# Block-causal attention and a gated feed-forward layer: other halves of PSUM share a tile in the last two seven-product stages, and the written-out order is searched anew

## The chip, the cores and the metric

The kernel runs on one core of a Trainium2 chip. The metric is the device time of one execution in microseconds; before the change it is 959.42 us, the median of three runs (957.42 to 960.23). Engines are called as in the profile: PE is TensorE (matmuls; PEld its weight loads), DVE is VectorE, ACT is ScalarE, POOL is GpSimd, SP is SyncE, which only issues DMA transfers. SPq and ACTq are the issues of transfers on SP's and ACT's queues.

## The reference

Inputs are q, k, v of shape (8, 8, 576, 64), w_in (512 x 2048) and w_out (2048 x 512). The output has 4608 x 512 elements.

```python
scores = scale * np.matmul(q, k.transpose(0, 1, 3, 2))      # scale = 1/8
scores = np.where(block_i >= block_j, scores, -1e9)         # blocks of 64 positions
attn = np.exp(scores - np.max(scores, axis=-1, keepdims=True))
attn = attn / (np.sum(attn, axis=-1, keepdims=True) + 1e-09)
x = np.matmul(attn, v)         # then heads side by side: 4608 x 512
h = x @ w_in
sp = np.where(h > 20.0, h, np.log1p(np.exp(np.minimum(h, 20.0))))
g = h * np.tanh(sp)
out = g @ w_out
```

## The kernel before

The 4608 tokens are nine tiles of 512 (b = 0 to 8). For each pair of heads the scores are computed (line 1499), their maxima taken (1544), the exponentials (1580) split into an fp16 high and low part (1624, 1631), transposed by DMA (1659, 1674) and multiplied by v (1714); a divide (1780, 1781) ends the attention of a pair, and further transposes (1967) turn the result into x. The weights arrive as pairs of 32-bit words, and DVE decodes them (825, 842); w_out comes in 16 chunks (816). ACT squares it (854), a matmul with ones, `over_rows` (748), sums the squares over the rows, and the scale found from it goes into the fp16 parts wo_h and wo_l (890, 902).

Both feed-forward matmuls are made of three fp16 products (high by high, high by low, low by high). For tiles 4 to 8 the first of them is done with seven products of half size in place of eight, as in Strassen's scheme (`m1_set`, 2182); tiles 7 and 8 do the second one so too (`m2_seven`, 2363), the others plainly (2530). In the seven-product scheme some operands are sums (S1 to S4) of blocks and some are blocks (A11, A12, A22), and the results are added up in PSUM and SBUF.

`m2_seven` works with three accumulators of 128 x 512 fp32, each a PSUM bank: X for A11 and later A12, Y for S2, then S3, then A22, Z for S1, then S4. PSUM tiles named `ss` are two banks wide, and there are two of them: X and Y are the halves of one, Z is in the other. A11, S2 and S1 are computed in four sets of 24 matmuls each over the inner dimension. Then, in this order on PE, come A12, S3, S4 and A22 (two halves of 24 matmuls), 48 matmuls each. Between them stand small operations: X is copied (`w1`, on ACT at 2401 or DVE at 2407), the copy is added into Y (`a1`, 2416), Y is copied (`cu`), Z is copied (`w2`), Y's copy is added into Z (`a2`), and the copy of Z and Y are added (`a3`). S3 begins when `cu` is done, S4 when `a2` is. The results leave by `out`: a scaled evacuation on DVE (2470) or ACT (2464) and a store (2494). The last one, of tile 8, is split into a half for DVE and a half for ACT, with the second half's store on ACT's queue.

The order of the work on every engine is written out. `AT` holds a due time for each operation, `WAY` one letter for each operation that several engines can do ("a", "d", "p"). `Plan.go` goes through the operations by due time with the costs that each was added with (a model of SP's queue among them: BEGIN, DONE, FLIGHT), and `order` emits them by the starts found so, per engine. The Tile framework then adds the semaphores: an instruction that touches a tile waits for the earlier ones on that tile which it must follow. A buffer ring (`ss_ring`, `work_ring`, ...) says when a tile may be taken again.

Of the kernel before, what the change touches and what calls it, by code (L numbers as in the profile page):

```python
# [358 lines left out]
class Plan:  # L359
# [5 lines left out]


    LAT, LATPE, OWN = 0.15, 0.2, 0.11

    FREE = 0.4

    BEGIN, DONE, FLIGHT = 0.65, 1.6, 8

    SWITCH = 1.3

    WINDOW, COLUMNS, SLOW, LEAD = 10.24 / 3, 3400, 1.93, 0.5

    def __init__(self):
# [20 lines left out]
    def go(self, due):  # L398
# [15 lines left out]
        while events:  # L414
            now = events[0][0]
            while events and events[0][0] <= now:
# [3 lines left out]
                o = ops[i]  # L420
# [2434 lines left out]
```

## Time and profile before

| | before |
|---|---|
| median of 3 runs | 959.42 us (957.42 to 960.23) |
| profiled execution | 958.82 us |
| its span | 956.9 us |
| mean granted PE clock | 0.998 |
| busy: PE / DVE / ACT / POOL | 937.5 / 764.6 / 605.4 / 280.6 us |

The span runs from the first to the last recorded instruction or transfer of the profiled execution; its own time is 1.9 us longer. A busy share close to the whole says which engine sets the pace; which stretch a change acts on is to be seen from the stretches, the waits and the chain that ended last.

### The profile page before, as it was taken

To read this page: it belongs to the slowest core of one execution; us is meant where nothing else is said; L and a number is where in the kernel's file an instruction comes from. 1 tells how busy PE (TensorE), PEld (TensorE's weight loads), DVE (VectorE), ACT (ScalarE), POOL (GpSimd) and SP (SyncE) were. 2 spreads that over 40 slices of the span, in tenths; PEclk is the share of its full clock that TensorE was granted. 3 is DMA by queue.
4 is the path that set the end of the run, shared out by engine and by line. 5 is a ranking of instruction groups with operands and counts; after the bars stand their busy time and mean duration, and the time that the engine had idled before them with its cause. 6 is when DMAs were issued, how large, how long until landed. Compare 5 with 4: busy or idle time off the path is not lost.

```text
span 956.9 us, 22382 instructions
## 1 busy us (share of the span) xinstructions
PE 937.5 (98%) x9060; PEld 616.5 (64%) x9060; DVE 764.6 (80%) x1445; ACT 605.4 (63%) x1021; POOL 280.6 (29%) x267
## 2 busy tenths in 40 slices
PE   8999998999999999999999999999999999999997
PEld 6777574545554555555557865786568747888886
DVE  7889998878789887766988886899768788984861
ACT  2739997568737884597667964688569424631540
POOL 0001211323335132233333605422575502201320
PEclk9999999999999999999999999999999999999999
DMA  8762889776664568866677769766886440014001
GB/s 293 245 204 95 190 179 216 165 161 130 139 128 98 136 147 170 164 141 160 138 155 147 149 135 181 143 155 147 162 180 106 81 102 17 13 40 105 1 1 45
DMA packets 298472, 128.35 MB, mean 134 GB/s; under 512 B 244608, under 2 KB 280704, under 8 KB 298368
## 3 DMA queue, kind: packets, MB, share of 16 engines
q1 hardware_dynamic: 298080, 126.49, 59.7%
q8 instruction: 71, 1.16, 0.5%
q10 hardware_dynamic: 288, 0.43, 0.1%
q14 instruction: 33, 0.27, 0.1%
HBM read 58.06 MB, written 10.49 MB: 72 GB/s over the span
## 4 chain that ended last, share of the span: by engine, by line
PE 90%; DVE 6%; DMA 2%; ACT 2%; issue 1%; SPq 0%; ACTq 0%; DVEq 0%
PE acc L2530 29%; PE acc L2182 18%; PE acc L2091 15%; PE ss L2363 8%; PE acc L1714 6%; PE ss L1499 6%; PE acc L1429 3%; PE ss L1358 1%; DVE sx L842 1%; DVE P L1631 1%; PE ss L1286 1%; DMA PT<-P 1%; DVE pv L1544 1%; DVE Gt L2040 1%; PE acc L1286 1%; PE acc L927 1%
## 5 line engine op out<-in xcount | busy, mean ns | idle before, releaser
L2530 PE MATMUL acc<-Gt,wo_h 128*128 128x512 f16 x896 | 267.9, 381 | 0.1
L2530 PE MATMUL acc<-Gt,wo_l 128*128 128x512 f16 x448 | 170.4, 380 | 0.0
L1580 ACT ACTIVATE pe<-ss,pv 128x192 f32<-128x192 f32 (+2 forms) x240 | 126.3, 608 | 59.0 <-DVE pv L1554 37.9
L2091 PE MATMUL acc<-x,wi_h 128*128 128x512 f16 (+2 forms) x640 | 156.9, 337 | 1.1 <-DVE many L1781 0.9
L2530 PEld LDWEIGHTS <-wo_h 128*128 128x128 f16 x896 | 82.5, 98 | 92.7 <-issue 7.2
L1544 DVE TENSOR_REDUCE pv<-ss 128x2 f32<-128x384 f32 (+4 forms) x140 | 104.5, 790 | 25.1 <-PE ss L1511 24.3
L1631 POOL TENSOR_TENSOR P<-pe,P 128x256 f16<-128x256 f32 (+3 forms) x67 | 83.4, 1266 | 120.2 <-DVE P L1624 48.7
L2182 PE MATMUL acc<-x,wi_h 128*128 128x256 f16 x640 | 108.0, 273 | 0.0
L2040 DVE SCALAR_TENSOR_TENSOR Gt<-F,bv,Gt 128x1024 f16<-128x1024 f32 (+2 forms) x80 | 96.3, 1216 | 11.6 <-ACT Gt L2028 9.2
L2091 PE MATMUL acc<-x,wi_l 128*128 128x512 f16 (+2 forms) x320 | 104.6, 336 | 0.0
L2091 PEld LDWEIGHTS <-wi_h 128*128 128x128 f16 x640 | 56.9, 98 | 49.8 <-issue 3.0
L2182 PE MATMUL acc<-x,wi_l 128*128 128x256 f16 x320 | 87.2, 273 | 0.0
L2182 PE MATMUL acc<-x,sx 128*128 128x256 f16 x720 | 86.6, 273 | 0.3 <-DVE acc L2226 0.3
L1714 PEld LDWEIGHTS <-PT 128*128 128x128 f16 x2128 | 72.2, 97 | 11.0 <-issue 1.4
L2530 PEld LDWEIGHTS <-wo_l 128*128 128x128 f16 x448 | 44.0, 98 | 53.4 <-issue 0.8
L2182 PEld LDWEIGHTS <-sx 128*128 128x128 f16 x720 | 69.8, 98 | 10.2 <-issue 0.8
L1631 DVE TENSOR_TENSOR P<-pe,P 128x256 f16<-128x256 f32 (+3 forms) x101 | 73.4, 769 | 1.8 <-ACT P L1624 1.6
L1714 PE MATMUL acc<-many,PT 128*128 128x65 f16 (+1 forms) x2128 | 74.3, 193 | 0.0
L1499 PE MATMUL ss<-many 64*128 64x64 f16 (+7 forms) x1280 | 73.7, 260 | 0.1
L2182 PEld LDWEIGHTS <-wi_h 128*128 128x128 f16 x640 | 61.9, 98 | 11.6 <-issue 1.0
L760 POOL TENSOR_SCALAR Gt<-F,bv 128x1024 f16<-128x1024 f32 (+2 forms) x26 | 33.4, 1285 | 105.3 <-ACT F L2119 58.5
L2235 ACT ACTIVATE F<-acc,bv 128x512 f32<-128x512 f32 x60 | 40.5, 686 | 23.2 <-PE acc L2182 20.6
(245 smaller groups left out, 1681.7 us busy)
## 6 DMA issues: line engine op xcount, KB each, us to landing
wo_l<-in_w_in_dram SPq DMA_DIRECT2D x8, 1024.0 KB, 6.4
sx<-in_w_out_dram SPq DMA_DIRECT2D x16, 512.0 KB, 4.6
many<-in_v_dram SPq DMA_DIRECT2D x28, 288.0 KB, 3.1
many<-in_k_dram SPq DMA_DIRECT2D x28, 288.0 KB, 3.3
many<-in_q_dram SPq DMA_DIRECT2D x28, 256.0 KB, 3.3
out_dram<-ot SPq DMA_DIRECT2D x28, 256.0 KB, 2.9
many<-in_v_dram SPq DMA_DIRECT2D x28, 192.0 KB, 3.5
many<-in_v_dram SPq DMA_DIRECT2D x28, 96.0 KB, 3.1
```

The lines of the kernel that those rows point to most:

```text
L760: nc.gpsimd.tensor_scalar(out=out, in0=x, scalar1=s, scalar2=1.0, op0=ALU.mult, op1=ALU.mult)
L1499: nc.tensor.matmul(ss[:, 512 * a + col : 512 * a + col + n], lhsT=m[q_][hs, at : at + P], rhs=m[k_][hs, key : key + n], start=first, stop= ...
L1544: nc.vector.reduce_max(out=mx[:, c], in_=ss[:, :, c0:c1], axis=mybir.AxisListType.X)
L1580: nc.scalar.activation(pe[ex[r].slot][:, cols], ss_[S0[r].slot][:, cols], AF.Exp, scale=esc, bias=mx[:, c, a : a + 1],)
L1631: eng.tensor_sub(l, x, h)
L1714: nc.tensor.matmul(out, lhsT=p_, rhs=v_, start=first, stop=True, skip_group_check=True,)
L2040: nc.vector.scalar_tensor_tensor(out=dst[:, 1], in0=src, scalar=self.s_g, in1=dst[:, 0], op0=ALU.mult, op1=ALU.subtract,)
L2091: nc.tensor.matmul(pt, lhsT=w[:, d, f * P : (f + 1) * P], rhs=rhs(x, d), start=k == 0 and d == 0 and z == 0, stop=d == NP - 1 and z == 2, ...
L2182: nc.tensor.matmul(pt[:, k * TH : (k + 1) * TH], lhsT=weights(kind, z, d, k), rhs=x_[:, d, blk, x, :], start=first and k == 0 and d == 0 a ...
L2235: lambda: nc.scalar.activation(dst(), src(), AF.Mish, scale=scale),
L2363: nc.tensor.matmul(pt[:, k * TH : (k + 1) * TH], lhsT=weights(kind, z, s, c, k), rhs=block(blk, x, s, c), start=one, stop=s == NS - 1 and ...
L2530: nc.tensor.matmul(pt, lhsT=w[:, f, o * P : (o + 1) * P], rhs=g, start=s == 0 and c == 0 and z == 0, stop=s == NS - 1 and c == FG - 1 and ...
```

## The change

Four things are changed. The table `AT` and the string `WAY` are replaced as a whole by those of a new search. The plan's model lets a long transfer on SP (over 1.4 us of issue, which are the transposes) hold the queue until what was sent before it has landed, and some costs of the model are smaller (`TURN`, `TURN_LATE`, `TURN_X`, the 0.12 of `over_rows`, now 0.03); these numbers only steer the order. In `m2_seven` X and Z now share a tile and Y has its own; in the last of the four sets the order is S1, A11, S2; A12 also waits for Z's copy `w2`, `a2` for A12, and S4 for the evacuation of X; the rings are released accordingly, and both halves of the last result wait for the whole of A22. The instructions on PE are the same in number and kind (9060 matmuls).

```diff
-    0, 20114, 1050, 475, 0, 4150, 3025, 1425, 950, 6938, 1900, 4832, 5885, 23380, 7413, 15638,
+    0, 12977, 1050, 0, 475, 5885, 2375, 1900, 3025, 4832, 10683, 950, 9630, 23859, 23209, 15050,
...
-    "adaadaaddaddapaadpapaaaaapdddaadpaapaddaadppddddaaapadpdadddaadadpdaaaapdddpddddapdaddpaaa"
+    "adaadpaadpaaaadadadpaaaaaadddpaapadaaadaapppddddapapapadadpdaadpdpddadappdadadadddpaddpadd"
...
@@ -369,6 +369,8 @@
     FREE = 0.4
 
     BEGIN, DONE, FLIGHT = 0.65, 1.6, 8
+
+    QUEUED = 1.4
 
     SWITCH = 1.3
 
@@ -458,6 +460,8 @@
                     locked = until[e] = max(until[e] - ops[i].tail, locked) + ops[i].tail
                 end[i] = until[e]
                 if e == "sp":
+                    if us > self.QUEUED:
+                        until[e] = max(until[e], moved + self.DONE)
                     flight += 1
                     moved = max(moved, until[e] + self.BEGIN) + ops[i].work
                     end[i] = moved + self.DONE
@@ -753,7 +757,7 @@
                 stop=True,
             )
 
-        o = add("pe", (0.12, 10.0), emit, after, [acc_ring])
+        o = add("pe", (0.03, 10.0), emit, after, [acc_ring])
         return o, lambda: acc_[o.slot][:, 0:n]
 
     def by_pool(out, x, s):
@@ -2418,19 +2422,20 @@
                     psum=True,
                 )
 
-            bx, bz = [None, 0], [None, 0]
+            bx, by, bz = [None, 0], [None, 0], None
             ends = {"A11": last["m2"], "S1": last["m2"]}
             for s in range(NS):
-                for kind, blk, bank in (("A11", 0, bx), ("S2", 5, None), ("S1", 3, bz)):
+                order = (("A11", 0, bx), ("S2", 5, by), ("S1", 3, bz))
+                for kind, blk, bank in order if s < NS - 1 else order[::-2] + order[1:2]:
                     if bank is None:
-                        bank = [bx[0], 1]
-                        ends.setdefault(kind, ends["A11"])
+                        bank = bz = [bx[0], 1]
+                    ends.setdefault(kind, ends["A11"])
                     free = [(p2_ring, self.rooms[2])] if kind == "S2" and s == NS - 1 else []
-                    ends[kind] = product(
-                        0, kind, blk, (s,), s == 0, [ends[kind]], bank, free=free
-                    )
+                    after = [ends[kind]]
+                    if kind == "A11" and s == NS - 1:
+                        after.append(ends["S1"])
+                    ends[kind] = product(0, kind, blk, (s,), s == 0, after, bank, free=free)
             p1, p6, p5 = (ends[x] for x in ("A11", "S2", "S1"))
-            by = [bx[0], 1]
             X, Y, Z = bank_of(bx), bank_of(by), bank_of(bz)
             w2 = []
             t = many[:, 4 * TN : 6 * TN].rearrange("p (a n) -> p a n", a=2)
@@ -2440,18 +2445,11 @@
             w1 = copy(W1[0], X, [p1] + [x for m in self.more for ops in m for x in ops])
             a1 = plus(Y, Y, W1[0], [w1, p6])
             cu = copy(W1[1], Y, [a1])
-            p2 = product(1, "A12", 1, every, False, [w1], bx)
+            w2.append(copy(W2[1], Z, [p1, p5], [work_ring]))
+            p2 = product(1, "A12", 1, every, False, [w1, w2[0]], bx)
             p7 = product(1, "S3", 4, every, False, [cu], by, free=[(p2_ring, self.rooms[1])])
-            w2.append(copy(W2[1], Z, [p5], [work_ring]))
-            a2 = plus(Z, Z, W1[1], [cu, w2[0]])
+            a2 = plus(Z, Z, W1[1], [cu, w2[0], p2])
             a3 = plus(W2[1], Y, W2[1], [w2[0], p7])
-            p3 = product(2, "S4", 2, every, False, [a2], bz)
-            p4 = [product(3, "A22", 6, every, False, [a3, p3], by, (0,))]
-            rooms = [(ot_ring, self.rooms[0])]
-            p4.append(product(3, "A22", 6, every, False, [p4[0]], by, (1,), rooms))
-            self.m2_begin = p3
-            self.reads = NS * [[p3] + p4]
-            last["m2"] = p4[1]
             stored = []
             self.evacs = []
 
@@ -2502,12 +2500,19 @@
 
             both = range(2)
             out(1, 0, 0, both, X, W1[0], [p2, a1], True, [], [])
+            p3 = product(2, "S4", 2, every, False, [a2, self.evacs[0]], bz)
+            p4 = [product(3, "A22", 6, every, False, [a3, p3], by, (0,))]
+            rooms = [(ot_ring, self.rooms[0])]
+            p4.append(product(3, "A22", 6, every, False, [p4[0]], by, (1,), rooms))
+            self.m2_begin = p3
+            self.reads = NS * [[p3] + p4]
+            last["m2"] = p4[1]
             out(2, 1, 1, both, W2[1], W2[1], [a3], False, [], [])
-            out(3, 0, 1, both, Z, W1[1], [p3, a2], True, [(ss_ring, bz[0])], [])
+            out(3, 0, 1, both, Z, W1[1], [p3, a2], True, [(ss_ring, bx[0])], [])
             last["tail"] = [x + [stored[0], stored[2]] for x in last["tail"]]
             for k in range(2):
                 out(
-                    3, 1, 0, (k,), Y, W2[0], [p4[k]], True, [(ss_ring, bx[0])] * k,
+                    3, 1, 0, (k,), Y, W2[0], [p4[1]], True, [(ss_ring, by[0])] * k,
                     [(work_ring, w2[0])] * k,
                 )
 
@@ -2734,8 +2739,8 @@
         return top, lo
 
     SLACK = 0.7
-    TURN, TURN_LATE = (2.7, 0.5), (1.25, 0.2)
-    TURN_X = {8: (1.4, 0.5), 12: (2.0, 0.5), 16: (2.7, 0.5), 24: (3.8, 0.9)}
+    TURN, TURN_LATE = (2.0, 0.5), (1.2, 0.2)
+    TURN_X = {8: (1.3, 0.5), 12: (1.5, 0.5), 16: (2.0, 0.5), 24: (2.9, 0.9)}
     heads, tiles, fars = [[], []], [], []
 
     own = [load_own(p) for p in range(NP)]
```

How the instructions move is shown at three places. Lines of the changed kernel are 4 or 5 higher (2416 is 2420). The first place is DVE at the end of tile 8, from the last split of the gated activations on. `ss_128` and `ss_129` are the two PSUM tiles. Before:

```order
1301 L2040 SCALAR_TENSOR_TENSOR Gt<-F_64,bv_120,Gt 128x1024
1302 L2407 COPY F_65<-ss_129 128x2x256
1303 L2416 TENSOR_TENSOR ss_128<-ss_128,many 128x512
1304 L2416 TENSOR_TENSOR ss_129<-ss_129,many 128x512
1305 L2470 TENSOR_SCALAR many<-ss_128,bv_120 128x256 x2
1306 L2416 TENSOR_TENSOR F_65<-ss_128,F_65 128x2x256
1307 L2470 TENSOR_SCALAR F_65<-F_65,bv_120 128x256 x2
1308 L2470 TENSOR_SCALAR F_65<-ss_128,bv_120 128x256
```

And now:

```order
1295 L2044 SCALAR_TENSOR_TENSOR Gt<-F_65,bv_120,Gt 128x1024
1296 L2420 TENSOR_TENSOR ss_129<-ss_129,many 128x512
1297 L2411 COPY many<-ss_129 128x2x256
1298 L2420 TENSOR_TENSOR ss_128<-ss_128,many 128x512
1299 L2420 TENSOR_TENSOR F_64<-ss_129,F_64 128x2x256
1300 L2468 TENSOR_SCALAR F_64<-ss_129,bv_120 128x256
```

The sum `a1` (Y and the copy of X) was on `ss_128`, the tile in which A12 accumulates, and is now on `ss_129`; `a2` (1304, now 1298) has gone to the tile of X. X's evacuation (1305) has gone to ACT, and the copy `cu` (1297) has come from there.

The second place is SP while the last chunks of w_out are loaded (DMA into `sx`); DMA_TRANSPOSE into `PT` are the transposes of the exponentials. Before, from the 14th chunk to the 16th:

```order
78 L816 DMA sx_76<-in_w_out_dram 128x4x256
79 L1659 DMA_TRANSPOSE PT_107<-P_102 128x16x128
80 L980 DMA many<-in_v_dram 128x576
81 L1100 DMA many<-in_q_dram 128x2x64
82 L816 DMA sx_75<-in_w_out_dram 128x4x256
83 L1659 DMA_TRANSPOSE PT_108<-P_103 128x16x128
84 L816 DMA sx_76<-in_w_out_dram 128x4x256
```

And now:

```order
77 L1663 DMA_TRANSPOSE PT_107<-P_102 128x16x128
78 L820 DMA sx_76<-in_w_out_dram 128x4x256
79 L1124 DMA many<-in_v_dram 64x128
80 L984 DMA many<-in_v_dram 128x576
81 L1124 DMA many<-in_v_dram 64x3x128
82 L820 DMA sx_75<-in_w_out_dram 128x4x256
83 L1663 DMA_TRANSPOSE PT_108<-P_104 128x16x128
84 L820 DMA sx_76<-in_w_out_dram 128x4x256
```

The three chunks are the 14th, 15th and 16th in both. The transpose `PT_107` has moved from behind the 14th chunk to ahead of it, and three loads of v stand between 14th and 15th.

The third place is the end of SP's queue, the last stores of tile 8 (the last half store is on ACT's queue and not here). Before:

```order
448 L2494 DMA out_dram<-F_65 128x256
449 L2494 DMA out_dram<-F_65 128x2x256
450 L2494 DMA out_dram<-many 128x2x256
451 L2494 DMA out_dram<-F_65 128x256
452 L2494 DMA out_dram<-F_65 128x2x256
453 L2494 DMA out_dram<-F_65 128x256
454 L2494 DMA out_dram<-many 128x2x256 x2
```

And now:

```order
449 L2492 DMA out_dram<-F_66 128x256
450 L2492 DMA out_dram<-F_66 128x2x256
451 L2492 DMA out_dram<-F_66 128x256
452 L2492 DMA out_dram<-many 128x2x256
453 L2492 DMA out_dram<-F_64 128x2x256
454 L2492 DMA out_dram<-many 128x2x256
455 L2492 DMA out_dram<-F_64 128x256
```

The store of 128x256 (128 KB, a half of the last result) stood ahead of two stores of 128x2x256 (256 KB each, one row with x2) and is now the last one on SP.

## Rows read from the trace of the kernel before

**Rows 1.** The page's first line and part 1.

```profile
span 956.9 us, 22382 instructions
...
PE 937.5 (98%) x9060; PEld 616.5 (64%) x9060; DVE 764.6 (80%) x1445; ACT 605.4 (63%) x1021; POOL 280.6 (29%) x267
```

**Rows 2.** Waits of PE: engine, line, releaser, us, times, longest.

```profile
...
PE acc L748 <- ACT wo_h L854: 2.4, 1, 2.4
PE ss L2363 <- DVE ss L2416: 2.2, 1, 2.2
PE ss L2363 <- DVE many L2407: 1.6, 1, 1.6
PE ss L2363 <- ACT many L2401: 1.5, 1, 1.5
PE acc L2091 <- DVE many L1781: 0.9, 1, 0.9
```

**Rows 3.** Stretches: us, busy per engine (instructions), PE clock, DMA share, GB/s.

```profile
...
160.00:162.90 2.90, 0.50 (x3) 0.10 (x2) 2.76 (x8) 2.05 (x3) 0.00 (x0) 1.00 1.11 221
...
164.20:167.60 3.40, 3.40 (x9) 1.22 (x8) 3.19 (x7) 3.40 (x6) 0.00 (x0) 0.51 1.17 175
167.60:834.00 666.40, 665.94 (x6558) 405.71 (x6557) 545.45 (x1022) 444.51 (x770) 241.02 (x221) 1.00 0.65 134
```

**Rows 4.** Timeline, PE: start, us, engine, what, [idle before, releaser].

```profile
...
857.85 0.38 PE L2363 MATMUL ss<-many,wo_h 128*128 128x256 f16 x2 [1.59 <-DVE many L2407]
858.45 0.28 PE L2363 MATMUL ss<-many,wo_l 128*128 128x256 f16 x1 [0.23 <-DVE wo_l L2714]
...
865.82 0.38 PE L2363 MATMUL ss<-Gt,PT 128*128 128x256 f16 x2 [2.17 <-DVE ss L2416]
...
935.58 0.38 PE L2363 MATMUL ss<-many,wo_h 128*128 128x256 f16 x2 [1.48 <-ACT many L2401]
```

**Rows 5.** Chain that ended last, 920 to 957: start, us, what.

```profile
...
921.00 13.11 PE ss L2363 x120
...
934.21 0.71 DVE ss L2416
...
934.94 0.59 ACT many L2401
...
935.58 15.89 PE ss L2363 x144
```

**Rows 6.** Timeline, DVE, tile 7's seven-product stage.

```profile
...
863.69 0.88 DVE L2470 TENSOR_SCALAR many<-ss,bv 128x256 f32<-128x256 f32 x2 [2.42 <-PE ss L2363]
...
865.08 0.69 DVE L2416 TENSOR_TENSOR ss<-ss,many 128x512 f32<-128x512 f32 x1
```

**Rows 7.** The tail: timeline of issues, then issues with us to landing.

```profile
...
952.52 0.92 SPq L2494 DMA_DIRECT2D out_dram<-many  x2
952.58 0.36 ACTq L2494 DMA_DIRECT2D out_dram<-F  x1
...
out_dram<-many SPq DMA_DIRECT2D x2, 256.0 KB, 2.8
out_dram<-F SPq DMA_DIRECT2D x1, 128.0 KB, 1.8
out_dram<-F ACTq DMA_DIRECT2D x1, 128.0 KB, 2.5
```

**Rows 8.** Timeline, SP and then DVE, while w_out is loaded.

```profile
...
142.31 4.89 SPq L1659 DMA_TRANSPOSE PT<-P  x1
...
149.51 0.41 SPq L816 DMA_DIRECT2D sx<-in_w_out_dram  x1
...
153.81 0.52 SPq L816 DMA_DIRECT2D sx<-in_w_out_dram  x1
...
154.01 0.43 DVE L825 TENSOR_SCALAR sx<-sx 128x512 int32<-128x512 int32 x1 [2.45 <-DMA sx<-in_w_out_dram]
...
158.94 0.42 DVE L825 TENSOR_SCALAR sx<-sx 128x512 int32<-128x512 int32 x1
```

More of the change, by code (lines that the diff above doesn't have):

```diff
@@ L321 @@
 WAY = (
-    "adaadaaddaddapaadpapaaaaapdddaadpaapaddaadppddddaaapadpdadddaadadpdaaaapdddpddddapdaddpaaa"
-    "adaapppadapadpaadddpapdddpdpaddadpdaapaaapadadaaadppaaappadaaaapppdpdaddddaaadddapdaapddpd"
-    "ppdddaddpdpdadddddpdpdadaaapaddadpdadddadppapddpapdddaddpddpdpddpppddpdpdddapdddddddapddda"
-    "pdppddpaddddpdaaadpddapddpppddaddpdappdpdadpapadaddpadppadpadpdadappdpadaaddpaaddpdaaddada"
-    "adadaadaapdadadaapddaddpapddppdpdadapdapadppaappaappdddadppdpdpdaaadpdddpdadappadaapdaaaaa"
-    "padapapdadpdadpdppddapdddpppadppadpddappaadadadadappppapaaapadadapdaaapaadaadaaadpdadadapa"
-    "dpppapppapaadpddpdpapadpppppadpdppppdppaaaddddaddddppdpadddadddpadpddapddadddadpdpaddddddd"
-    "daddddddddaddddpdddadddadddpadaaadddapdpapaaddddapddaaaaaddpappddaaaadddaadaaaadaddaaddddd"
-    "ddadddpdpddddaaddppppadaaadpddapdpaadaddpdaapaapaaadddaadaapaaddda"
+    "adaadpaadpaaaadadadpaaaaaadddpaapadaaadaapppddddapapapadadpdaadpdpddadappdadadadddpaddpadd"
+    "ddaapapappdaaddaappddddddddddpdpddddadpapdadaddaapaaddaaddaddaaadddapddddaadapadapdaadddpd"
+    "pdpdddadppapapdpaaadaaapppdadadadddappdaddppppdpaddpdddddadddaddddppdppadppdddppddddappdpp"
+    "dpdaddpapppdadapaadapppdadadapadpdaapddppadpadddapapdddpaddadadaaapdddapdadpdaddppaadppada"
+    "daaaaaaadadpdaddaaadadapapdadpdpppppaddpddppadppaapddpddaaddddadadapddaddpdaaaaaadpaaadapd"
+    "pddapapddpapadddddaapddddpdaapppppppadapappddadadadppdddaaddpadapdddappdaadaaaaaapdpdapapa"
+    "dapadpappdaddppdpddaaadpppdpaadaddppdadadaddddadddpaddpddddpddpdaddddaddpddddadppdaddddadd"
+    "paddpddpddaddpdadddaddpaddddpdadaddddppaadaaddddaapaaadaadpdaapaaadaddddaadaaaaaaddddadapd"
+    "ppaddaddppdpaadpddaadppadaadpdapdpaaaadpddaapadpaaadddaapdaaadaaaa"
 )
```

566 rows, old and new, of the table AT are left out of this document.

## The prediction, made before the changed kernel was run

> **What bounds the kernel now.** I read the page first: a span of 956.9 us in which TensorE is busy for 937.5, 98% [rows 1]. TensorE is therefore the bound, and the whole room is what it does not spend at its full pace: 19.4 us idle, plus whatever it loses to a lower clock. Other engines matter where TensorE waits for them. The list of TensorE's waits [rows 2] puts the idle time down to few places: three waits of the seven-product stage (line 2363) for a sum or a copy, 2.2, 1.6 and 1.5 us; one of 2.4 at line 748, where the sum over w_out's rows waits for ScalarE's squares; one of 0.9 at line 2091 for a divide; the rest is below half a microsecond each, but for the wait for the first load of q, which opens the span. The table of stretches [rows 3] then says where in time that is: between 167.6 and 834.0, 70% of the span, TensorE is busy 665.94 of 666.40 us, so nothing is to be had there; around 160 to 168 there is first a gap and then 3.4 us at a granted clock of 0.51, the lower level of 1.2 GHz.
>
> **The waits of the seven-product stage.** Their size at the start of the next matmul is more than the idle column, since the ends of pipelined matmuls are modelled: a 128x256 matmul alone is booked as 0.27, and in a pair as 0.38, so the step is 0.11 (13.11 us for 120 in the chain [rows 5] gives 0.109). Each wait thus costs its idle time plus 0.27 - 0.11 = 0.16: 1.59 + 0.16 = 1.75 at 857.85, 0.23 + 0.16 = 0.39 at 858.45, 2.17 + 0.16 = 2.33 at 865.82, 1.48 + 0.16 = 1.64 at 935.58 [rows 4]. The sum is 6.1 us.
>
> What makes them is read in the chain around 934 [rows 5]. TensorE runs 120 matmuls up to 934.12; the last 48 are the product A12, which adds into X. Only then does VectorE's sum into Y start (934.21, 0.71 us), then ScalarE's copy (934.94, 0.59), and then S3 (935.58). The operands of that sum were complete when A12 began, 48 x 0.109 = 5.2 us earlier. It waited because X and Y are halves of one PSUM tile: the framework holds a reader or writer of a tile for the last writer of the tile, not of the half. Tile 7 has it the same way, and there again in front of S4: X's evacuation waits 2.42 us at 863.69 although A12 ended at 856.3 (857.85 less the 1.59 idle ahead of it [rows 4]), because S3 writes Y in the same tile; the sum into Z at 865.08 stands behind it on VectorE [rows 6].
>
> **What the change makes of them.** X and Z share a tile now, Y has its own. The sum into Y waits for S2 and the copy of X, and both are there when A12 starts; sum and copy (0.71 + 0.59 = 1.3) run beside A12's 5.2 us. X's evacuation (0.88) and the sum into Z (0.69) wait for A12 and run beside S3's 5.2 us. The price is a new wait: A12 writes the tile that Z is in, so it also waits for the copy of Z. In the last set S1 and A11 now come ahead of S2, so both copies (0.59 each, 1.18 on one engine) have S2's 24 matmuls, 24 x 0.109 = 2.6 us, to hide in. S4 waits for X's evacuation as well: 0.88 + 0.69 = 1.57 against 5.2. All four covers are more than twice what they hide, the count of matmuls is the same, and no new dependence reaches further. Queued behind the sum into Y on VectorE are only this stage's own sums and evacuations in tile 8; in tile 7 also weight sums, which now start earlier, not later. Term A: -6.1; bounds -6.1 and, if one of the two copies lies behind something else on its engine, -6.1 + 1.6 (the size of the smallest of the three larger waits) = -4.5.
>
> The Trainium skill, page "PSUM — Partial Sum Buffer", section "PSUM bank collisions raise a hardware error", says that two engines must be kept apart on the same bank and quadrant of partitions, so that halves in two banks need no guard. By that rule alone pairing the halves anew would gain nothing, as X, Y and Z have a bank each before and after. The trace differs: the sum into one bank started 0.09 us after the last matmul into the other. What each would give is the second rival below.
>
> **The tail.** After the last matmul (951.48) VectorE and ScalarE evacuate a half each; then two 256 KB stores go out on SP at 952.52 and 128 KB on ScalarE's queue at 952.58. The 256 KB stores take 2.8 from issue to landing, a 128 KB store on SP at the same moment 1.8, the one on ScalarE's queue 2.5 [rows 7]. One of the two large stores is Z's, ready long before, and it stands behind the small store on SP that waits for VectorE. In the new order the large stores stand ahead of that wait and only the two 128 KB stores are left at the end. The second large one is issued half way through the row's 0.92, at 952.98, and lands at 952.98 + 2.8 = 955.8; the last small one would land at 952.58 + 1.8 = 954.4. Term B: -1.4; the lower bound is -0.7, if ScalarE's queue takes its 2.5 whatever runs beside it (955.1).
>
> **w_out's load.** The gap at 160.3 to 162.9 costs 2.40 + 0.16, and the 3.4 us at 0.51 that follow [rows 3] cost half of 3.4 = 1.7: together 4.3. Behind it stands ScalarE's Square, which waits for VectorE's last decode of w_out. VectorE in turn waited 2.45 us up to 154.01 for the 15th of 16 chunks, issued on SP at 149.51 [rows 8]. Ahead of that issue SP was held 4.89 us by a transpose (142.31). In the new order this transpose stands ahead of the 14th chunk, and none is left between 14th and 15th; between 15th and 16th one is left, as before. On VectorE the work ahead of the last decode is shorter by 3.7 us by the durations of before (its instructions up to there in either order, each with the mean of its kind); the matmul that needs the result comes 14 matmuls of 0.03 = 0.4 us earlier. If both loads come earlier by the hold, the wait and the slow clock behind it go: -4.3. If the 16th chunk stays where it is, it lands at 153.81 + 4.5 = 158.3 and is decoded at 158.94, so only 0.6 can be won; if it is late by a further hold, 4.9 is lost. I take -2.5, the middle of -4.3 and -0.6, as the rows speak for one chunk and are silent on the other. Term C: -2.5, bounds -4.3 and +4.9.
>
> **The new order elsewhere.** The same instructions in another order on all engines; the summed busy time by the durations of before is within 1 us on VectorE, 6 us more on ScalarE and 4 less on POOL, and none of the three is the bound. The present order leaves a wait of 0.9 (line 2091 [rows 2]) and 0.46 idle in 666 us. The new one cannot win more than these 1.4. What it can lose is bounded by one hold of 4.89 on SP [rows 8] that ends as a wait of TensorE. I take one further wait like the present 0.9, the nearest row of this kind. The wait for the first load I leave as it is, since loads of q and k still open the queue. Term D: +0.9, bounds -1.4 and +4.9.
>
> **Sum.** -6.1 - 1.4 - 2.5 + 0.9 = -9.1 on the profiled execution's 958.82 gives 949.7. That execution is 0.6 below the median of the three runs, so the forecast is 950.3.
>
> **Rivals.** First, the waits go in the late tiles but are given back while the weights are loaded: A and B hold (-7.5), C is 0 and D +4.9, so 959.4 - 2.6 = 956.8, and 953 to 957 with C between. For it: SP's share is highest there and every transfer order is new. Against: 167.6 to 834 shows that the present order copes almost everywhere.
>
> Second, the pairing has no effect: what held the sum into Y was something else that ends with A12 (by the page's rule there is nothing between the banks to hold it), and it is still there. Then A is 0 and the rest -1.4 - 2.5 + 0.9 = -3.0, or near 0 with C at 0: 956.4 to 959, centre 958. For it: X and Y have been in different banks all along. Against: the evacuation of X at 863.69 waited through all of S3, which writes Y alone, though X's own last writer had ended at 856.3: the tile is what they share.
>
> Third, slower: the transposes' hold on SP. The change counts the queue as held until earlier transfers have landed, and moves loads ahead of transposes and behind them accordingly; where that puts values or keys of a pair behind a transpose, each costs up to 4.89 us of SP (142.31) and the scores wait. One such hold that TensorE feels is paid by A, two by A, B and C; from the third on the kernel is slower: 3 x 4.89 - 7.5 = +7.2, 966.6. For it: the loads of all later pairs stand among the transposes of the earlier ones. Against: with the present mixture, and VectorE at 80% [rows 1], TensorE waited 0.46 us in 666 [rows 3], so such holds are covered by work on hand nearly everywhere.
>
> **How the numbers follow.** Less than about 0.3%, 2.9 us, can't be told from no change here: faster is below 956.5, slower above 962.3. Chances: forecast with its own spread, 945.5 (C at -4.3, D at -1.4, B at its full size) to 954, 0.70; first rival 0.14, of which two thirds lie below 956.5; second 0.10, nearly all of it same; third 0.06. That gives faster 0.70 + 0.10 + 0.02 = 0.82, same 0.12, slower 0.06. The range that holds 8 in 10 runs from 945.8 to 956.8: it takes in the bounds of C and D on the good side and one uncovered hold on the other.
>
> **What would show it.** In the changed kernel's list of TensorE's waits the three rows of the seven-product stage must be gone; VectorE's sum into Y must start within 0.2 us of S2's last matmul and run beside A12; A12 must start right after S2, else the copy of Z is late. In the tail the last two stores must be the 128 KB ones. Around the sum over w_out's rows the wait should be near or below 1 and the stretch at 0.51 shorter or gone; a wait of 2 there with a clock of 0.5 would put C at 0. A wait at lines of values or scores of 4 us or more in the first 170 us would be the first or third rival. A sum into Y that still begins with A12's end would be the second and would make the forecast wrong by all of A.

## The result and the profile after

The changed kernel takes 948.9 us, the median of four runs (947.19 to 950.93), against 959.83 before; the ratio is 0.9889 with a 95% interval of 0.9859 to 0.9918. The forecast was 950.3, with a range of 945.8 to 956.8.

The profiled execution took 950.93 us and is the longest of the four; the other three had a mean granted clock of 1.000 where it had 0.998. Its first line and part 1, which answer to [rows 1]:

```profile
span 949.2 us, 22388 instructions
...
PE 934.4 (98%) x9060; PEld 616.0 (65%) x9060; DVE 775.1 (82%) x1439; ACT 611.2 (64%) x1031; POOL 284.1 (30%) x265
```

TensorE's busy time fell by 3.2 us (937.54 to 934.35) although it runs the same 9060 matmuls, and its idle time by 4.6 (19.4 to 14.8). Where the idle time is left is told by the list of TensorE's waits (engine, line, releaser, us in total, times, longest):

```profile
PE acc L752 <- ACT wo_h L858: 2.1, 1, 2.1
PE ss L1400 <- DVE PT L1333: 1.9, 1, 1.9
PE acc L2095 <- DVE many L1785: 1.0, 1, 1.0
PE ss L1503 <- ACT pe L1584: 0.6, 2, 0.3
```

No row of the seven-product stage is left; before there were four, 2.2, 1.6, 1.5 and 0.2 us [rows 2, 4]. The wait at the sum over w_out's rows is still there (2.1 for 2.4), the one at a divide (line 2095) has moved from 127 to 432, and the one at line 1400, near the start, is new. The first load of k takes the place of q's (4.7 for 4.5).

The stretches show the same, in the same columns as [rows 3] (us, busy per engine, PE clock, DMA share, GB/s):

```profile
162.90:164.20 1.30, 1.30 (x4) 0.45 (x3) 0.74 (x4) 1.30 (x1) 1.10 (x2) 0.50 1.22 272
164.20:167.60 3.40, 3.40 (x59) 2.27 (x58) 2.35 (x1) 2.20 (x5) 0.00 (x0) 0.92 1.06 155
167.60:834.00 666.40, 664.39 (x6512) 403.98 (x6509) 558.26 (x1032) 449.12 (x774) 234.05 (x209) 1.00 0.64 134
834.00:870.00 36.00, 36.00 (x333) 32.27 (x331) 27.89 (x38) 10.88 (x16) 9.75 (x8) 1.00 0.36 78
```

TensorE is busy in all 36.00 us of tile 7's stretch. The lower level of the clock still follows the wait at w_out, a little earlier. From 167.6 to 834 the idle time has grown from 0.46 to 2.01 us.

The end of the chain of waits (start, us, what), which answers to [rows 5]:

```profile
913.81 31.45 PE ss L2367 x288
...
945.29 0.49 DVE F L2468
...
945.81 0.47 ACT F L2462
```

The 288 matmuls of tile 8's seven-product stage run in one piece at 0.109 us each; VectorE and ScalarE no longer stand in the chain until the last evacuation. How that comes is seen in the timeline of VectorE, then ScalarE, at this place (idle time before, releaser in brackets):

```profile
924.39 0.70 DVE L2420 TENSOR_TENSOR ss<-ss,many 128x512 f32<-128x512 f32 x1 [1.82 <-PE ss L2367]
925.13 0.69 DVE L2411 COPY many<-ss 128x512 f32<-128x512 f32 x1
929.62 0.70 DVE L2420 TENSOR_TENSOR ss<-ss,many 128x512 f32<-128x512 f32 x1 [3.80 <-PE ss L2367]
...
921.83 0.59 ACT L2405 COPY many<-ss 128x512 f32<-128x512 f32 x1 [3.62 <-PE ss L2367]
922.31 0.59 ACT L2405 COPY F<-ss 128x512 f32<-128x512 f32 x1
930.36 0.84 ACT L2462 ACTIVATE many<-ss,bv 128x256 f32<-128x256 f32 x2 [7.46 <-DVE ss L2420]
```

S2's last matmul ends at about 924.3 (96 matmuls of 0.109 after 913.81), and the sum into Y starts at 924.39, beside A12. Before, it started when A12 had ended. Both copies of ScalarE (921.83, 922.31) are done by 922.9, inside S2's last 24 matmuls. The sum into Z (929.62) and X's evacuation (930.36 to 931.2) follow A12 and end well before S3 does, at about 934.8.

The tail, issues and then us to landing, answers to [rows 7]:

```profile
945.80 0.34 SPq L2492 DMA_DIRECT2D out_dram<-F  x1
...
946.31 0.35 ACTq L2492 DMA_DIRECT2D out_dram<-F  x1
...
out_dram<-many SPq DMA_DIRECT2D x1, 256.0 KB, 2.6
out_dram<-F SPq DMA_DIRECT2D x1, 128.0 KB, 1.8
out_dram<-F ACTq DMA_DIRECT2D x1, 128.0 KB, 1.8
```

The last two issues are the 128 KB stores, and ScalarE's takes 1.8 here where it took 2.5 beside the large ones. From the start of the last matmul to the end of the span it is 4.18 us (5.75 before).

While w_out is loaded, SP, then VectorE, then ScalarE (answering to [rows 8]):

```profile
142.62 0.54 SPq L820 DMA_DIRECT2D sx<-in_w_out_dram  x1
...
145.12 0.55 SPq L820 DMA_DIRECT2D sx<-in_w_out_dram  x1
...
148.64 0.43 DVE L829 TENSOR_SCALAR sx<-sx 128x512 int32<-128x512 int32 x1 [1.36 <-DMA sx<-in_w_out_dram]
...
152.05 0.90 DVE L829 TENSOR_SCALAR sx<-sx 128x512 int32<-128x512 int32 x1
...
158.69 1.91 ACT L858 ACTIVATE wo_h<-sx 128x2048 f16<-128x2048 f32 x1 [0.88 <-DVE sx L846]
```

The 15th chunk is issued at 145.12 instead of 149.51, and VectorE no longer waits for it (152.05 has no idle time ahead); it waits 1.36 for the 14th. ScalarE's square starts at 158.69 instead of 160.85.

To add it up, the span is cut at matmuls that have the same number in both orders, with the starts in the trace of before, after, and the changed kernel's second profiled execution (below):

| piece | before | after | after, second |
|---|---|---|---|
| to the 1553rd matmul (the sum of line 1150 in the changed kernel) | 169.83 | 168.06 | 165.18 |
| from there to the 8101st | 670.55 | 672.22 | 672.38 |
| from there to the last | 110.81 | 104.70 | 104.69 |
| from its start to the span's end | 5.75 | 4.18 | 4.16 |

So in the first profiled execution -1.8, +1.7, -6.1 and -1.6, which is -7.8 in all, in the second -4.7, +1.8, -6.1 and -1.6, -10.5 in all. The third piece and the tail are the same in both; the first differs by 2.9 us.

What the first piece won in the first execution is not waiting. The stretch up to the 1553rd matmul, before and after, in the columns of [rows 3]:

```profile
0.00:169.83 169.83, 161.83 (x1553) 113.41 (x1554) 149.20 (x323) 121.95 (x193) 18.75 (x29) 0.99 0.76 203
0.00:168.06 168.06, 159.18 (x1553) 113.00 (x1554) 147.12 (x315) 120.75 (x193) 26.63 (x38) 0.99 0.79 207
```

TensorE's busy time falls by 2.7 us here and its idle time grows by 0.9. About half of the 2.7 lies in the first twelve matmuls of line 1358 (now 1362), 2.91 and 1.59 us, which stand just ahead of the new wait of 1.9; the rest was not taken apart.

### The profile page after: what moved, and what is told of

Its sections match the earlier page's. It is cut to its first block, busy times and chain, and to the rows that moved or that the text cites. A ratio compares the mean times of both kernels' runs of the same rounds, so it can differ in the third digit from the quotient of the medians.

```text
span 949.2 us, 22388 instructions
## 1 busy us (share of the span) xinstructions
PE 934.4 (98%) x9060; PEld 616.0 (65%) x9060; DVE 775.1 (82%) x1439; ACT 611.2 (64%) x1031; POOL 284.1 (30%) x265
## 4 chain that ended last, share of the span: by engine, by line
PE 90%; DVE 4%; ACT 3%; DMA 2%; issue 1%; POOL 0%; SPq 0%; ACTq 0%; DVEq 0%; POOLq 0%
PE acc L2535 28%; PE acc L2186 19%; PE acc L2095 15%; PE ss L2367 8%; PE acc L1718 7%; PE ss L1503 6%; PE acc L1433 3%; DVE pv L1548 1%; PE ss L1362 1%; ACT pe L1584 1%; DMA many<-in_v_dram 1%; PE ss L1290 1%; DMA wo_l<-in_w_in_dram 1%; PE acc L931 1%; PE ss L1400 1%
## 5 line engine op out<-in xcount | busy, mean ns | idle before, releaser
L1635 POOL TENSOR_TENSOR P<-pe,P 128x256 f16<-128x256 f32 (+3 forms) x84 | 98.3, 1195 | 138.0 <-ACT P L1628 78.0
L1628 POOL CAST P<-pe 128x256 f16<-128x256 f32 (+3 forms) x44 | 32.5, 759 | 133.3 <-ACT pe L1584 113.4
L1635 DVE TENSOR_TENSOR P<-pe,P 128x256 f16<-128x256 f32 (+3 forms) x84 | 65.5, 817 | 5.7 <-POOL P L1628 3.5
```

Of the source, the lines that this page charges most:

```text
L1628: op(out=h, in_=x)
L1635: eng.tensor_sub(l, x, h)
```

## Experiments

Lines of `AT` below are due times in thousandths of a microsecond; within one engine they are ranks. Kernels that were timed ran beside the kernel before, and ratios are to it.

**The old pairing in the new order (e1_pair_undone).**

```diff
-bx, by, bz = [None, 0], [None, 0], None
+bx, by, bz = [None, 0], None, [None, 0]
-                        bank = bz = [bx[0], 1]
+                        bank = by = [bx[0], 1]
 # and the rings: Z's evacuation frees bz, the last one frees bx
```

> The changed kernel with its new order, but Y again shares a PSUM tile with X, and Z has its own. If the pairing alone removes the four waits of the seven-product stages, all of them come back: TensorE waits some 1.75 + 0.39 + 2.33 us in tile 7 and 1.64 in tile 8, 6.1 us in all, and the time is near 955. If part of it was the order on VectorE (in tile 7 the evacuation of X stood ahead of the sum into Z, now it stands behind it), only the two waits at the start of S3 come back, 1.75 and 1.64, so +3.4 us, and S4 of tile 7 starts at once. If the pairing has no effect, +0.

Measured: 951.56 us (951.23 to 953.38), ratio 0.9918 (0.9897 to 0.9938). TensorE's waits in the seven-product stage:

```profile
PE ss L2367 <- ACT many L2405: 3.0, 3, 1.5
PE ss L2367 <- DVE many L2411: 1.6, 1, 1.6
```

The piece from matmul 8101 to the last is 109.91, 5.2 more than in the changed kernel. The whole time is only 2.7 above the changed kernel's 948.9, since this execution was shorter in the two pieces that the edit does not touch (164.26 and 671.67), as were those of e3_no_cover and e4_stores_last, run beside it. Neither theory has it right. The waits at S3 came back as both said (1.5 and 1.6); the one at S4 of tile 7 did not, since the sum into Z now stands ahead of X's evacuation on VectorE, so that one belonged to the old pairing and the old order together. In its place there is a wait that neither named, 0.7 and 0.8 us ahead of A12. The timeline of ScalarE and then VectorE in tile 7:

```profile
843.41 0.58 ACT L2405 COPY F<-ss 128x512 f32<-128x512 f32 x1
845.35 0.58 ACT L2405 COPY many<-ss 128x512 f32<-128x512 f32 x1 [1.35 <-PE ss L2367]
...
852.80 0.70 DVE L2420 TENSOR_TENSOR ss<-ss,many 128x512 f32<-128x512 f32 x1 [5.97 <-PE ss L2367]
```

Z's copy (843.41) is made in time, but X's waits until 845.35 for S2's last matmul, because S2 writes the other half of X's tile; A12 starts behind it. The sum into Y then waits 5.97 us for A12, as before. Two accumulators in different banks still wait for each other: it is the tile that holds, which the second rival denied.

**The new pairing in the old order (e2_pair_alone).** The function `m2_seven` of the changed kernel in the kernel before, with the old due times given to the same operations, and:

```diff
+AT[3227], AT[3228], AT[3225], AT[3229] = 841215, 842531, 843847, 845163  # tile 7: S1, A11, S2, S2
+AT[3233] = 844500      # tile 7: Z's copy, ahead of A12
+AT[3260] = 849700      # and 3261 to 3264: sums of another stage that held the buffer it needs
+AT[3410], AT[3411], AT[3408], AT[3412] = 914911, 916227, 917543, 918859  # tile 8
```

> The kernel before with the new pairing of X, Y and Z and the new dependences, its old order kept but for the last sets of these products (S1 and A11 ahead of S2), the copy of Z and, in tile 7, three sums of another stage that held the buffer which that copy needs. If the pairing is the cause, the waits of 1.6, 2.2, 1.5 and 0.2 us at the seven-product line are gone from the list of waits and the time falls by 6.1 us, to about 953.5; the start, the wait for w_out and the tail stay as they were. If the rest of the new order is what counts, the gain is under 3 us.

Measured: 953.72 us (952.14 to 954.65), ratio 0.9933 (0.9908 to 0.9958), which is -6.4 us of 960.38 (-8.8 to -4.0). The waits at the sum over w_out's rows and in the seven-product stage:

```profile
PE acc L788 <- ACT wo_h L894: 2.4, 1, 2.4
...
PE ss L2403 <- DVE ss L2456: 0.5, 1, 0.5
```

The wait for w_out is as before; of the four waits at the seven-product line one is left, 0.5 at S4 of tile 7, behind VectorE's sum into Z, whose place on VectorE is the old one. The last piece of matmuls is 105.32, 5.5 less than before. So the pairing with its dependences makes 5.5 of the 6.1 us without the order that the search found elsewhere, and the new order takes away the wait that is left. The tail did not stay quite as it was: 6.13 us for 5.75, with ScalarE's last store at 3.2 to landing for 2.5.

**The copies uncovered (e3_no_cover).**

```diff
+AT[3224], AT[3225], AT[3229], AT[3227], AT[3228] = 835359, 836675, 837991, 839307, 840623
+AT[3408], AT[3412], AT[3410], AT[3411] = 910371, 911687, 913003, 914319
```

> The changed kernel with S2's last two sets moved ahead of the last set of S1 and A11, so that nothing stands between A11 and A12. Theory: the 24 matmuls of S2 (2.6 us) hide the two copies that A12 now waits for; without them A12 waits for both copies, 2 x 0.59 us and their starts, about 1.3 us in each of tiles 7 and 8, +2.6 us in all, listed at the seven-product line with ScalarE's copy as the releaser. Rival: the framework lets A12 begin as soon as X's own copy is there (the bank counts, not the tile): about 0.7 us each, +1.4.

One execution, 949.23 us. The waits in the seven-product stage:

```profile
PE ss L2377 <- ACT F L2415: 1.3, 1, 1.3
PE ss L2377 <- ACT many L2415: 1.2, 1, 1.2
```

They stand in front of A12 in tiles 8 and 7 (in tile 8 Z's copy is ScalarE's second and is waited for, in tile 7 X's own, so that tile 8 alone speaks against the rival). The last piece of matmuls takes 107.45, 2.8 more than in the changed kernel, against 2.6 expected and 1.4 by the rival. A12 does wait for both copies, and S2's last 24 matmuls are what hides them.

**The large stores last (e4_stores_last).**

```diff
+AT[3422], AT[3427] = 937950, 937945   # X's and the copy's stores behind the first half's
```

> The changed kernel with its last small store on SP put ahead of the two large stores of tile 8, as it was before. Theory: the span then ends 1.4 us later after TensorE's last matmul (5.4 instead of 3.95 us). Rival: the tail is set by ScalarE's queue, whose last store takes 2.5 whatever stands on SP: then the end moves by 0.7 or less.

One execution, 947.74 us. The last issues on SP and the us to landing:

```profile
941.48 0.43 SPq L2495 DMA_DIRECT2D out_dram<-F  x1
...
941.96 0.50 SPq L2495 DMA_DIRECT2D out_dram<-many  x1
...
out_dram<-many SPq DMA_DIRECT2D x1, 256.0 KB, 2.9
out_dram<-F SPq DMA_DIRECT2D x1, 128.0 KB, 1.8
out_dram<-F ACTq DMA_DIRECT2D x1, 128.0 KB, 2.5
```

From the last matmul's start to the end it is 5.69 us, against 4.16 and 4.18: +1.5, and 5.75 before. ScalarE's store took 2.5 again. The order of the stores is worth the whole of term B. That this execution is nevertheless shorter than the changed kernel's median comes from the first two pieces, which the edit does not touch: 164.29 and 671.28, where a0_after below has 165.18 and 672.38.

**The changed kernel again (a0_after).** No edit.

> The changed kernel once more, beside the kernel before and the three variants of this set on the same chip. Expected 0.989 of the kernel before. In its profiled execution 3.4 us ran at half the clock after a wait of 2.1 us; three other executions had a mean clock of 1.000. If that stretch comes and goes, executions with a mean clock of 0.998 should be some 2 us longer than those of 1.000.

Measured: 948.05 us (946.73 to 948.47, six runs), ratio 0.9889 (0.9864 to 0.9915). Two of its waits, and the stretch behind the sum over w_out's rows:

```profile
PE acc L752 <- ACT wo_h L858: 1.0, 1, 1.0
PE ss L1400 <- DVE PT L1333: 1.0, 1, 1.0
...
160.00:168.00 8.00, 8.00 (x108) 4.93 (x107) 7.07 (x17) 7.31 (x12) 1.72 (x2) 1.00 1.00 183
```

Here the wait at the sum is 1.0 instead of 2.1 and the clock stays at 1.00. The 2.9 us between the two profiled executions are all in the first piece of the table: 1.2 until the sum starts (160.74 and 159.51), and 1.7 from there, which is half of the 3.4 us at the lower level that followed the longer wait. None of the six executions had a mean clock of 0.998, so the expected difference in time between the two kinds rests on the traces alone.

**The sum over w_out's rows later (e5_sum_later).**

```diff
+AT[330] = 161130      # was 158733
```

> The changed kernel with the sum over w_out's rows moved behind nine more matmuls of 128x512 and fourteen small ones on TensorE (2.4 us of work that needs nothing of it). Theory: the sum starts when it did, since its input sets it, but TensorE works until then: the wait of 2.1 us shrinks to 0.3 or less, and with it the stretch at half the clock, so -2.1 to -3.8 us against the profiled execution of the changed kernel and -1 to -2 against its median. Rival: the work is only lent, and the next step (the split of w_out, VectorE's line 906) is then waited for: the wait moves there, gain under 1 us.

Measured: 948.35 us, ratio 0.9893 (0.9865 to 0.9921): no gain. The wait at the sum is gone from the list, and these are new:

```profile
PE acc L2537 <- DVE pv L732: 0.8, 1, 0.8
...
PE acc L754 <- DVE many L1787: 0.4, 1, 0.4
```

The first ends at 167.6, the second at 165.3, at the 1553rd matmul, which starts at 165.29 against 165.18 in the changed kernel beside it. The rival is right in that the work was lent. The split of w_out is not itself the releaser, but it stands in the way: VectorE does it from 165.15 for 2.34 us (line 908), and the small operation of line 732 for which TensorE waits comes right behind it.

**The start (e6_decode_later, e7_both, e9_first_loads).** e6 has the first line, e7 that and the edit of e5, e9 both lines.

```diff
+AT[30] = 10500                              # first decode of w_in, was 9630
+AT[7], AT[8], AT[11] = 950, 1000, 2700      # second pair's q and k, third pair's q
```

> The changed kernel with VectorE's first decode of w_in put behind the first pair's maxima, as in the kernel before. Theory: the wait of 1.86 us at the start (TensorE for VectorE's line 1333) is due to that decode, which waits for a load of w_in that lands at 9.6; without it in front the wait goes, and what is late next is the second pair's load of q, landing at 10.5: gain 1.3 to 1.9 us. Rival: the loads set the start whatever the order, TensorE waits as long in front of the next matmuls: gain under 0.5.

> The changed kernel with both moves (sum over w_out's rows later on TensorE, first decode of w_in later on VectorE). If the two are independent the gains add: 3 to 4 us below the changed kernel's median, about 945. If work ahead of the sum then comes earlier by the first gain and the squares do not, the wait at the sum grows by that much and only one of the two is left: 946 to 947.

> The changed kernel with VectorE's first decode behind the first pair's maxima and the second pair's q and k loaded ahead of w_in, as in the kernel before. Theory: the waits at the start go (0.4 to 1.9 us here), and if the start counts, the time falls by as much against the changed kernel, to about 946.5. Rival: the decodes of w_out are a second chain through the first 160 us that TensorE meets at the sum over w_out's rows, so that what the start wins is waited for there: the time stays at 948 and the wait at the sum is longer by the gain.

Measured: 947.84 us for e6 (0.9889, 0.9864 to 0.9914), 948.19 for e7 (0.9889, 0.9863 to 0.9914), 948.08 for e9 (0.9878, 0.9859 to 0.9897). None differs from the changed kernel. In e6 the loads and the sum over w_out's rows:

```profile
PE acc L1292 <- DMA sx<-in_k_dram: 5.9, 2, 4.6
...
PE acc L754 <- ACT wo_h L860: 1.0, 1, 1.0
```

The second of its two waits for a load is 1.2 us, for the second pair's k: the wait moved one step on. In e9 neither is left behind the first load (4.9), and the sum over w_out's rows reads:

```profile
159.83 0.16 PE L757 MATMUL acc<-wv,consts 128*128 128x2 bf16 x1 [1.23 <-ACT wo_h L863]
```

TensorE is done with what stands ahead of the sum at 158.6, no earlier than in a0_after (159.51 less the wait of 1.00 is 158.5), and the 1553rd matmul starts at 165.49. The rival of e9 has the time right and the place wrong: TensorE is 0.4 us ahead of a0_after at its 40th matmul and no longer at its 100th, at 16 us. Nothing won at the start came as far as w_out, so these runs do not show that w_out's decodes would have taken it back. No version that beats the changed kernel came out of this.

**The hold of the transpose alone (e8_hold_moved).** The kernel before with

```diff
+AT[692] = 141700      # transpose ahead of the 14th chunk of w_out, was 143099
```

> The kernel before with one transposing load of SP moved: it stands ahead of the 14th chunk of w_out instead of behind it, as in the changed order; nothing else is different. If the hold of 4.89 us between the 14th and the 15th chunk is what makes the sum over w_out's rows late, the transpose takes some 3 us in its new place, the 15th chunk is issued about 2.4 us earlier, VectorE's wait of 2.45 us for it goes, TensorE's wait at the sum shrinks from 2.4 to between 0 and 1.7 (the 14th chunk is later instead), and the time falls by 1 to 4 us, the more if the stretch at half the clock goes too. If VectorE's own work sets the sum, nothing moves.

Measured: 959.84 us, ratio 1.0003 (0.9988 to 1.0019). TensorE's wait at the sum, SP's transpose and its 14th and 15th chunk, and VectorE's wait for the 14th and its decode of the 15th:

```profile
PE acc L750 <- ACT wo_h L856: 2.0, 1, 2.0
...
140.75 3.37 SPq L1661 DMA_TRANSPOSE PT<-P  x1
144.22 0.53 SPq L818 DMA_DIRECT2D sx<-in_w_out_dram  x1
...
147.23 0.42 SPq L818 DMA_DIRECT2D sx<-in_w_out_dram  x1
...
149.14 0.43 DVE L827 TENSOR_SCALAR sx<-sx 128x512 int32<-128x512 int32 x1 [1.46 <-DMA sx<-in_w_out_dram]
...
154.03 0.89 DVE L827 TENSOR_SCALAR sx<-sx 128x512 int32<-128x512 int32 x1
```

The transpose is shorter in its new place (3.37 for 4.89) and the 15th chunk is issued 2.3 us earlier, as expected; but the 14th comes later (144.22 for 141.83), VectorE waits 1.46 for it, and it comes to the 15th at 154.03 with no wait, where before it came at 154.01 after one of 2.45. Its own work has taken the place of the wait, and TensorE's wait only falls from 2.4 to 2.0. The hold is therefore not what sets the sum by itself. In this execution the clock dropped twice, behind this wait and in tile 7. The second drop (stretch, us, PE busy, clock, DMA share, GB/s):

```profile
866.00:870.00 4.00, 4.00 (x26) 0.62 0.18 41
```

It is behind the wait of 2.2 in tile 7, at which the kernel before kept 1.00 in its profile. In this execution it costs more than the 0.4 that the wait at the sum won; the median of ten shows no gain either.

## Why the prediction was right

**Term A, the four waits (-6.1).** Measured -6.1 in the traces, 5.5 of idle time and 0.6 of busy time, as the 0.16 added to each wait had it. The step "the tile is what they share" holds: giving only the pairing takes 5.5 us off (e2_pair_alone), taking only the pairing away gives 5.2 back (e1_pair_undone). The cover counted for the new wait, S2's last 24 matmuls, is needed and enough: 2.8 us without it, nothing with it. One step was read too simply. The wait of 2.33 at S4 of tile 7 was put down to the pairing; it needs the old rank of two operations on VectorE as well.

**Term B, the tail (-1.4).** Measured -1.6, and +1.5 when the stores are put back. The lower bound, that ScalarE's queue is slow by itself, fell: its store took 1.8 with nothing large beside it and 2.5 with it.

**Term C, w_out (-2.5, bounds -4.3 and +4.9).** This is the weak term. The wait fell by 0.3 in the first profiled execution and the slow stretch stayed, which by the prediction's own sign (a wait of 2 with a clock of 0.5) puts C at about 0; in the second the wait fell by 1.4 and the stretch went, 3.1 together. The second kind is the usual one by the mean granted clock: 0.999 or 1.000 in 9 of the 10 executions of the changed kernel, at most 0.998 in 29 of the 30 executions of the kernel before (of 955 to 965 us) beside the experiments. The whole piece up to the 1553rd matmul, in which this term lies with the new wait at the start, the divide that moved out of it and the busy time that the prediction had no term for, gave -1.8 and -4.7. The hold ahead of the 15th chunk, alone, is worth nothing measurable (e8_hold_moved). What the new order did besides on VectorE and SP that brought the square 2.2 us forward was not taken apart, and stays open. The order alone does not settle it: up to 830 us e1_pair_undone and e4_stores_last have the same instructions in the same order on every engine as the changed kernel, and in the four traces (after, a0_after, e1, e4) SP issues the 14th chunk at 142.62, 141.77, 141.09 and 140.82, TensorE waits 2.1, 1.0, not at all and 0.2 at the sum, and the 1553rd matmul starts at 168.06, 165.18, 164.26 and 164.29.

**Term D, the order elsewhere (+0.9, bounds -1.4 and +4.9).** From the 1553rd to the 8101st matmul +1.7 to +1.8: the wait at a divide is still one of 1.0 but lies in this piece now, and there are more small ones beside it. The start also got worse, by a wait at line 1400 of 0.3 to 1.9 us, which the prediction left at nothing ("loads of q and k still open the queue"): not the loads but VectorE's decode of w_in, put ahead of the pair's maxima, made it. Its removal won nothing (e6_decode_later, e9_first_loads): the second pair's k was waited for instead, or the lead was gone by 16 us. The busy times were misreckoned too: VectorE has 10.5 us more where the prediction had it within 1, POOL 3.5 more where it had 4 less; neither engine is the bound.

**The rivals.** The second (the pairing without effect) and the third (holds on SP that make the kernel slower) did not happen. The first did in part: something was given back, 1.7 us, but after the loading phase and a third of what it asked for; and its condition that C is 0 was met in the first profiled execution.

**The sum.** A and B, 7.5 of the 9.1 us, are right in mechanism and size. That the total came so near is partly luck: C went from 0 to -3 between two executions of the same code, D is twice its +0.9, and the forecast's -9.1 lies between the -7.8 and the -10.5 of the two traces. One end of the spread is also added up wrongly: 945.5 should be 946.2 by the prediction's own terms (959.4 - 6.1 - 1.4 - 4.3 - 1.4).

## What to carry to other kernels

Two accumulators that live in halves of one tile are one object to whoever adds the waits: give a tile to those whose last writer and next reader come together, and check what the next product now has to wait for, and what work covers that. A wait of an engine at 98% is worth its length only where nothing else is late just behind it; here four waits at the end of the program were worth all of their 6.1 us, and those of the loading phase that the runs shortened or took away (e5 to e9) none that could be measured, since in the traces the next load, sum or decode was late in their place.

## What the runs showed of the hardware

A wait of TensorE of about 2 us was followed by some 3.4 us at half the clock in some executions and not in others: after 2.4 us at w_out it was (before, [rows 3]), after 2.1 and 2.0 too (after, e8_hold_moved), after 1.0 not (a0_after); after 2.2 in tile 7 it was in one profile (0.62 over 866 to 870, e8_hold_moved) and not in that of the kernel before. Such a stretch is 1.7 of the 2.9 us by which the two profiled executions of the changed kernel differ. A 128 KB store on ScalarE's queue took 1.8 us by itself (after) and 2.5 with two stores of 256 KB issued on SP at the same time (before, e4_stores_last), 3.2 in e2_pair_alone. A DMA transpose held SP's queue for 4.89 us behind the 14th chunk of w_out, and for 3.37 when that one row was moved ahead of it (before, e8_hold_moved).
